# Second expert layer: the seventh product before the sixth and third, and the first block of hidden units used first

## The chip, the cores and the metric

The kernel runs on one core of a Trainium2 chip. A core has a matrix engine (TensorE, called PE in the profile, with its weight loads as PEld), a vector engine (DVE), a scalar engine (ACT), GpSimd (POOL) and a queue that issues transfers (SP). The metric is the device time of one execution, in microseconds. Three runs of the kernel before gave 748.62 us as their median (748.35 to 753.33).

## The reference

Attention over 2 x 8 heads and 576 positions with a memory term gives 1152 tokens of 512 numbers. A feed-forward layer (512 to 2048 units, squared ReLU, back to 512) follows, and then four experts that all see every token:

```python
x = x @ w_in; g = np.maximum(x, 0)**2; x = g @ w_out
for e in range(4):
    h = np.maximum(x @ w1[e], 0.0)        # 512 -> 1024 units
    out += p[:, e:e + 1] * (h @ w2[e])    # 1024 -> 512
```

The result is float32. The change touches the experts alone.

## The kernel before

The experts are computed in two chunks of tokens: 4 tiles of 128 tokens (chunk 0), then 5 tiles (chunk 1). In each chunk a loop goes over 4 experts and 4 quarters of each expert's hidden units, 32 steps in all, numbered 0 to 31 here; steps 0 to 15 are chunk 0. A quarter has 256 units, in two blocks m = 0 and m = 1 of 128.

The first layer of a step (`up2`, from line 872) is a product of a 2 x 2 block matrix (units by inputs) and a 2 x 2 block matrix (inputs by halves of the tokens) in seven block products instead of eight. Products are numbered 0 to 6. Each is six matmuls of 256 columns (320 in chunk 1), because a float32 operand is held as two float16 parts and three pairings are multiplied (`PASS`). Sums on VectorE and GpSimd join the products: p1 from product 0, u2 from product 4, p5 from product 3, u4 = u2 + p5 (on GpSimd), and then
- h[0], the first block of units: its left half is product 1 + p1, its right half product 6 + u4;
- h[1], the second block: its right half is product 5 + u4, its left half product 2 + u3, where u3 is product 5 + u2.

When both halves of a block are there, `hidden(m)` (line 895) makes its two float16 parts: ReLU on ScalarE (L898), then on VectorE the rest (L899), both named g. The order of the products before is 0, 1, 4, 3, 5, 2, 6; I call them by place, U1 to U7. So block 1 is finished after U6 and block 0 after U7.

The second layer of a step (`down2`, line 959) takes g as weights: per token tile and block three matmuls of 512 columns into the bank `o` of that tile (L975), accumulated over the four quarters of an expert and then drained to a sum by VectorE (`drain`, L986/L988). Before, it takes block 1 for all tiles first and then block 0: eight groups D1 to D8 in chunk 0, ten in chunk 1.

The main loop (after line 999) runs the second layer of step i - 1 among the first layer of step i. TensorE's order is the written order: U1 U2 D1 U3 D2 D3 U4 D4 U5 D5 D6 U6 D7 U7 D8 in chunk 0, then U1 of the next step. So g of step i - 1 is first needed at D1, two products after the end of step i - 1. In the last product of step 0 the last groups of the layer ahead (y, L670) stand in place of the D groups; its four blocks are copied out by ScalarE (L676) and VectorE (L677) before the banks can become `o`.

The products of the first layer go round through accumulation banks (`spots`, line 750): four of them in chunk 0, three in chunk 1. A bank is free when ScalarE or VectorE has read the product. Now and then a small product (`yt`, `wt`) takes a place in that round.

ScalarE, VectorE, GpSimd and SP don't run in written order: a scheduler puts the instructions of each engine in a row when the program is built, and each engine runs its row strictly in order. In these rows also stand the splitting of the next weights (`wu` L847, L852 and L858; `w` L782 and L783; `ws` on GpSimd), the sums of squares (`junk`, L779) that wait for the transfer of a weight block (`raw`, L836), and the preparation of chunk 1's tokens (`xs` and `tt`, one piece at the end of each step from step 5 on). A `raw` buffer is loaded again when the split of the block in it has been made.

Of the kernel before, what the change touches and what calls it, by code (L numbers as in the profile page):

```python
# [52 lines left out]
def attention_then_experts(ctx, tc, qa, ka, va, qc, kc, vc, mz, beta, w1, probs, w2, out):  # L53
# [698 lines left out]
    def bank(shape, name):  # L752
        turn[0] += 1
        pool, tag = spots[turn[0] % len(spots)]
        return pool.tile(shape, F32, tag=tag, name=name)
# [116 lines left out]
    def up2(i):  # L872

        c = pairs[i][0]
        n = width[c]
        w = wus.pop(i)

        def product(k):
            acc, x = bank([P, n], "pe"), xs[c][k]
            m = 0  # L880
            for kk in range(2):
                for wa, xb in PASS:
                    nc.tensor.matmul(  # L883
                        acc, lhsT=w[:, wa, k, kk * P:kk * P + P], rhs=x[:, xb, kk], start=(m == 0), stop=(m == 5)
                    )
                    m += 1
            return acc

        def term(tag):
            return xp.tile([P, n], F32, tag=tag, name=tag, bufs=1)  # L890

        h = [xp.tile([P, 2, n], F32, tag=f"h{m}", name=f"h{m}", bufs=1) for m in range(2)]
        p1, p5, u2, u3, u4 = (term(tag) for tag in ("p1", "p5", "u2", "u3", "u4"))

        def hidden(m):
            g = gs[i, m] = xp.tile([P, 2, 2 * n], F16, tag=f"g{m}", name=f"g{m}")
            hm = h[m].rearrange("p j n -> p (j n)")
            nc.scalar.activation(out=g[:, 0], in_=hm, func=AF.Relu)  # L898
            nc.vector.scalar_tensor_tensor(  # L899
                out=g[:, 1], in0=hm, scalar=0.0, in1=g[:, 0], op0=ALU.max, op1=ALU.subtract  # L900
            )

        def add(out, acc, x):
            nc.vector.scalar_tensor_tensor(out=out, in0=acc, scalar=HID, in1=x, op0=ALU.mult, op1=ALU.add)  # L904

        nc.scalar.activation(out=p1, in_=product(0), func=AF.Copy, scale=HID)
        yield
        add(h[0][:, 0], product(1), p1)
        yield
        add(u2, product(4), p1)  # L910
        yield
        nc.scalar.activation(out=p5, in_=product(3), func=AF.Copy, scale=HID)  # L912
        nc.gpsimd.tensor_add(u4, u2, p5)  # L913
        yield
        acc = product(5)
        add(u3, acc, u2)
        add(h[1][:, 1], acc, u4)
        yield
        add(h[1][:, 0], product(2), u3)
        hidden(1)  # L920
        yield
        add(h[0][:, 1], product(6), u4)
        hidden(0)
        yield

    def chain(*gens):
# [3 lines left out]
    with tc.tile_pool(name="ps_3", bufs=1, space=PSUM) as ps_3, tc.tile_pool(name="gp2", bufs=2) as gp2:  # L930
        side, up_0 = chain(tokens(0, nc.gpsimd), prep_up(0)), None
        for i, _ in enumerate(ffn1(2, ps_3, gp2, 2)):
            if i == 6:
                y_power(0, ps_e.tile([P, NK], F32, tag="b", name="yt"))
            if 8 <= i < 56 and i % 4 == 0:
                fetch((i - 8) // 8, i // 4 % 2)
            if 36 <= i < 84 and i % 6 == 0:
                square((i - 36) // 12, i // 6 % 2)
            if i == 90:
                w_power(0, ps_e.tile([P, 8], F32, tag="d", name="wt").rearrange("p (m n) -> p m n", m=2))  # L940
            if (16 <= i < 72 and i % 8 == 7) or (i >= 104 and i % 4 == 3):
                next(side, None)
            if i >= 8 * n1 - 8:
                up_0 = up_0 or up2(0)
                next(up_0, None)
        run(up_0)
# [12 lines left out]
    def down2(i):  # L959

        c, e, p = pairs[i]
        t0, t1 = EXPERT_CHUNKS[c]
        if p == 0:
            scale = prs[c, e] = acp.tile([P, t1 - t0], F32, tag="prs", name="prs", bufs=2)
            nc.vector.tensor_scalar(
                out=scale, in0=pr[:, t0:t1, e], scalar1=winv[:, e:e + 1], scalar2=ypow[:, c, 1:2], op0=ALU.mult, op1=ALU.mult
            )
            for t in range(t0, t1):
                outs[t] = ps_o.tile([P, DM], F32, tag=f"o{t - t0}", name="o")
        todo = [(t, m) for m in (1, 0) for t in range(t0, t1)]  # L970
        for t, m in todo:
            g, w = gs[i, m], wds[i, m]
            r = (t - t0) * P
            for k, (wa, gb) in enumerate(PASS):
                nc.tensor.matmul(  # L975
                    outs[t], lhsT=g[:, gb, r:r + P], rhs=w[:, wa],
                    start=(p == 0 and m == 1 and k == 0), stop=(p == 3 and m == 0 and k == 2),
                )
            if p == 3 and m == 0:
                drain(t, e, t - t0, prs[c, e][:, t - t0:t - t0 + 1])  # L980
            yield

    def drain(t, e, i, scale):
        if e == 0:
            acc[t] = acp.tile([P, DM], F32, tag=f"acc{i}", name="acc")
            nc.vector.tensor_scalar_mul(acc[t], outs[t], scale)  # L986
        else:
            nc.vector.scalar_tensor_tensor(  # L988
                out=acc[t], in0=outs[t], scalar=scale, in1=acc[t], op0=ALU.mult, op1=ALU.add
            )  # L990
        if e == ne - 1:
            r = 0
            for b, r0, n in TILES[t]:
                nc.sync.dma_start(out=out[b * S + r0:b * S + r0 + n, :], in_=acc[t][r:r + n])
                r += n
# [4 lines left out]
    for i in range(len(pairs)):  # L1000
        if pairs[i][0] and len(spots) > 3:
            spots.pop()

        fetch(i + 6, 0)
        fetch(i + 6, 1)
        todo = iter([(j, half) for j in {0: (), 1: (4, 5), 2: (6, 7)}.get(i, (i + 5,)) for half in range(2)])
        if i:
            late = [down2(i - 1)] * (2 * (EXPERT_CHUNKS[pairs[i - 1][0]][1] - EXPERT_CHUNKS[pairs[i - 1][0]][0]))
            steps = spread([up2(i)] * 7, late, 0.25)
        else:  # L1010
            steps = []
        ahead = chain(prep_down(i), prep_up(i + 1))
        for n, g in enumerate(steps):
            next(g)
            next(ahead, None)
            if n in (5, 7, 9, 11):
                square(*next(todo, (len(pairs), 0)))
            if n == 10 and i == 1:
                y_power(1, bank([P, NK], "yt"))
                side = tokens(1, nc.vector)  # L1020
            if n == 14 and i < 4 * ne - 4 and i % 4 == 2:
                w_power(pairs[i + 2][1], bank([P, 8], "wt").rearrange("p (m n) -> p m n", m=2))
        if i >= 5 and steps:
            next(side, None)
        run(ahead)
    run(down2(len(pairs) - 1))


# [58 lines left out]
```

## Time and profile before

| | |
|---|---|
| median of three runs | 748.62 us |
| the profiled execution, its own time | 746.23 us |
| its span, first to last instruction | 744.4 us |
| granted TensorE clock, mean | 0.968 |
| TensorE busy | 698.9 us, 94% of the span |
| VectorE busy | 581.7 us, 78% |

The span is 1.83 us shorter than the execution's own time, which holds what lies around it. The experts take the span from about 371 us on; chunk 0 ends at about 538 us. In the views, "idle before" is the time that an engine stood still ahead of an instruction, and the name behind the arrow is what came last. Overlapping rows of one engine are pipelined.

### The profile page before, as it was taken

How to read it: one execution, taken by the hardware profiler on the slowest of the kernel's cores; microseconds unless marked ns; L12 is line 12 of the kernel's file. 1: busy time of each engine (PE TensorE's matmuls, PEld its weight loads, DVE VectorE, ACT ScalarE, POOL GpSimd, SP SyncE). 2: the span in 40 equal slices, each digit the busy share in tenths (PEclk: the TensorE clock that was granted, in tenths of full speed). 3: DMA queues.
4: the chain of work that ended last, by engine and by line, in shares of the span. 5: the costliest groups of instructions: out<-in, count | busy, mean ns of one | idle time of the engine just before them, and what ended most of it. 6: DMA issues, size and time to landing. Idle time of an engine off the chain costs nothing.

```text
span 744.4 us, 12986 instructions
## 1 busy us (share of the span) xinstructions
PE 698.9 (94%) x4732; PEld 507.2 (68%) x4732; DVE 581.7 (78%) x1081; ACT 449.4 (60%) x888; POOL 295.5 (40%) x293
## 2 busy tenths in 40 slices
PE   8588999989899999989999989999999999999997
PEld 6487978967677887979876555656655555555553
DVE  5888989689989865666788879989787686867763
ACT  5798798686665545687775657645545353535341
POOL 1235536564533237745634243444323323141400
PEclk6779999999999999999999999999999999999999
DMA  8786675187975544685413223223342322100002
GB/s 301 223 302 234 215 240 199 62 283 217 205 190 121 121 114 93 233 291 162 135 59 114 86 85 114 91 81 114 114 148 81 112 70 100 58 1 1 1 1 71
DMA packets 65424, 101.28 MB, mean 136 GB/s; under 512 B 32656, under 2 KB 34704, under 8 KB 65360
## 3 DMA queue, kind: packets, MB, share of 16 engines
q1 hardware_dynamic: 65216, 100.45, 43.2%
q8 instruction: 37, 0.61, 0.3%
q14 instruction: 27, 0.22, 0.1%
q10 hardware_dynamic: 144, 0.00, 0.0%
HBM read 82.87 MB, written 10.75 MB: 126 GB/s over the span
## 4 chain that ended last, share of the span: by engine, by line
PE 35%; DVE 8%; ACT 4%; DMA 3%; issue 3%; POOL 2%; SPq 0%; DVEq 0%; POOLq 0%; ACTq 0%
PE o L975 18%; PE pe L883 16%; DMA raw<-in_w 2%; DVE wu L847 2%; DVE g L899 1%; DMA wraw<-w1s 1%; DVE h L904 1%; ACT junk L779 1%; DVE w L783 1%; POOL w L83 1%; ACT g L898 1%; ACT wu L852 1%; ACT w L82 1%; PE y L670 0%; DVE xs L783 0%
## 5 line engine op out<-in xcount | busy, mean ns | idle before, releaser
L975 PE MATMUL o<-w,g 128*128 128x512 f16 x864 | 219.5, 381 | 6.4 <-DVE g L899 3.9
L883 PE MATMUL pe<-xs,wu 128*128 128x256 f16 (+1 forms) x1344 | 198.6, 288 | 1.8 <-DVE h L904 1.8
L883 PEld LDWEIGHTS <-wu 128*128 128x128 f16 x1344 | 131.8, 99 | 71.0 <-issue 4.2
L975 PEld LDWEIGHTS <-g 128*128 128x128 f16 x864 | 84.1, 98 | 77.6 <-DVE g L899 6.8
L670 PE MATMUL y<-g,w 128*128 128x256 f32 (+2 forms) x576 | 125.3, 351 | 1.4 <-POOL w L83 0.7
L83 POOL TENSOR_TENSOR w<-wraw,w 128x512 fp32r<-128x512 f32 x49 | 72.6, 1485 | 100.8 <-ACT w L82 99.9
L898 ACT ACTIVATE g<-h 128x512 f16<-128x512 f32 (+1 forms) x64 | 43.4, 678 | 107.5 <-DVE h L904 107.4
L670 PEld LDWEIGHTS y<-g,w 128*128 128x128 f32 x576 | 94.5, 191 | 12.0 <-POOL w L83 0.9
L913 POOL TENSOR_TENSOR u<-u,p 128x256 f32<-128x256 f32 (+1 forms) x32 | 31.5, 986 | 135.2 <-ACT p L912 126.7
L899 DVE SCALAR_TENSOR_TENSOR g<-h,g 128x512 f16<-128x512 f32 (+1 forms) x64 | 50.8, 793 | 21.5 <-ACT g L898 21.3
L850 POOL TENSOR_TENSOR ws<-raw 128x256 f32<-128x256 f32 x32 | 23.9, 746 | 99.6 <-issue 86.6
L904 DVE SCALAR_TENSOR_TENSOR h<-pe,u 128x256 f32<-128x256 f32 (+1 forms) x96 | 43.0, 451 | 21.6 <-PE pe L883 16.2
L89 PE MATMUL hpb<-xy,w 128*128 128x512 f32 x192 | 52.9, 412 | 4.9 <-DVE r L660 4.8
L847 DVE SCALAR_TENSOR_TENSOR wu<-ws,wpow,wu 128x512 f16<-128x512 f32 x64 | 52.0, 850 | 3.2 <-ACT wu L858 3.1
L783 DVE SCALAR_TENSOR_TENSOR w<-raw,wpow,w 128x512 f16<-128x512 f32 x64 | 48.2, 755 | 0.7 <-ACT w L782 0.6
L172 DVE CUSTOM_DVE_ANT_0 a<-sc,mask 128x384 f32<-128x384 f32 (+4 forms) x80 | 36.4, 477 | 13.5 <-PE sc L275 7.9
L82 ACT ACTIVATE w<-wraw 128x512 fp32r<-128x512 f32 x64 | 39.5, 622 | 10.6 <-PE y L670 6.9
L89 PEld LDWEIGHTS hpb<-xy,w 128*128 128x128 f32 x192 | 36.1, 196 | 14.1 <-DVE r L660 6.6
L782 ACT ACTIVATE w<-raw,wpow 128x512 f16<-128x512 f32 x64 | 45.0, 709 | 0.5 <-PE o L975 0.5
L83 POOL TENSOR_TENSOR w<-bits,w 128x512 fp32r<-128x512 f32 x24 | 35.3, 1477 | 20.8 <-ACT w L82 17.5
L89 PE MATMUL hpa<-xy,w 128*128 128x256 f32 x192 | 37.3, 320 | 6.0 <-DVE xy L200 3.7
L779 ACT ACTIVATE junk<-raw 128x1024 bf16<-128x1024 f32 x32 | 33.5, 1048 | 14.8 <-DMA raw<-in_w 14.7
(161 smaller groups left out, 1264.6 us busy)
## 6 DMA issues: line engine op xcount, KB each, us to landing
raw<-in_w SPq DMA_DIRECT2D x64, 512.0 KB, 3.3
w<-in_w SPq DMA_DIRECT2D x32, 512.0 KB, 4.1
wraw<-w1s SPq DMA_DIRECT2D x64, 256.0 KB, 2.9
w1s<-bits SPq DMA_DIRECT2D x32, 256.0 KB, 2.5
kraw<-in_kc SPq DMA_DIRECT2D x8, 576.0 KB, 4.2
vraw<-in_vc SPq DMA_DIRECT2D x8, 320.0 KB, 3.6
qraw<-in_qc SPq DMA_DIRECT2D x4, 512.0 KB, 4.7
out<-acc SPq DMA_DIRECT2D x8, 256.0 KB, 2.1
```

Of the source, the lines that this page charges most:

```text
L82: nc.scalar.activation(out=w[:, 0], in_=raw, func=AF.Copy)
L83: eng.tensor_sub(w[:, 1], raw, w[:, 0].bitcast(F32))
L89: nc.tensor.matmul(acc, lhsT=w[:, a, kk * P:(kk + 1) * P], rhs=xy[:, b, kk, t0:t0 + n], start=(i == 0), stop=(i == 3 * NK - 1),)
L670: nc.tensor.matmul(yacc[d], lhsT=w[:, a, d * P:(d + 1) * P], rhs=g[:, b], start=(f == 0 and i == 0 and d % per == 0), stop=(f == n1 - 1 an ...
L782: nc.scalar.activation(out=w0, in_=x, func=AF.Copy, scale=s)
L783: nc.vector.scalar_tensor_tensor(out=w1, in0=x, scalar=s, in1=w0, op0=ALU.mult, op1=ALU.subtract)
L847: nc.vector.scalar_tensor_tensor(out=w[:, 1, ks], in0=x, scalar=s1, in1=w[:, 0, ks], op0=ALU.mult, op1=ALU.subtract)
L883: nc.tensor.matmul(acc, lhsT=w[:, wa, k, kk * P:kk * P + P], rhs=x[:, xb, kk], start=(m == 0), stop=(m == 5))
L898: nc.scalar.activation(out=g[:, 0], in_=hm, func=AF.Relu)
L899: nc.vector.scalar_tensor_tensor(out=g[:, 1], in0=hm, scalar=0.0, in1=g[:, 0], op0=ALU.max, op1=ALU.subtract)
L904: nc.vector.scalar_tensor_tensor(out=out, in0=acc, scalar=HID, in1=x, op0=ALU.mult, op1=ALU.add)
L975: nc.tensor.matmul(outs[t], lhsT=g[:, gb, r:r + P], rhs=w[:, wa], start=(p == 0 and m == 1 and k == 0), stop=(p == 3 and m == 0 and k == 2),)
```

## The change

Product 6, with the add that finishes h[0] and with `hidden(0)`, is taken in the fifth place; products 5 and 2 follow. The order of the products is 0, 1, 4, 3, 6, 5, 2. The second layer takes block 0 for all tiles first and then block 1, and the flags that open and close the accumulation, and the place of the drain, go with it. No instruction is added or removed.

```diff
         nc.gpsimd.tensor_add(u4, u2, p5)
         yield
+        add(h[0][:, 1], product(6), u4)
+        hidden(0)
+        yield
         acc = product(5)
         add(u3, acc, u2)
         add(h[1][:, 1], acc, u4)
         yield
         add(h[1][:, 0], product(2), u3)
         hidden(1)
         yield
-        add(h[0][:, 1], product(6), u4)
-        hidden(0)
-        yield
...
-        todo = [(t, m) for m in (1, 0) for t in range(t0, t1)]
+        todo = [(t, m) for m in (0, 1) for t in range(t0, t1)]
...
-                    start=(p == 0 and m == 1 and k == 0), stop=(p == 3 and m == 0 and k == 2),
+                    start=(p == 0 and m == 0 and k == 0), stop=(p == 3 and m == 1 and k == 2),
                 )
-            if p == 3 and m == 0:
+            if p == 3 and m == 1:
```

The scheduler makes other rows of it. VectorE at the end of step 0, where the layer ahead ends (pe_4472, pe_4486, pe_4488 and pe_4502 are products of step 0, y0 to y3 the four blocks of the layer ahead, wu_4607 the next weights but one), before:

```order
L904 SCALAR_TENSOR_TENSOR h1_4418<-pe_4472,u4_4423 128x256
L677 TENSOR_TENSOR xy_75<-y0_3696,xy_75 128x384
L904 SCALAR_TENSOR_TENSOR h1_4418<-pe_4486,u3_4422 128x256
L677 TENSOR_TENSOR xy_75<-y1_3697,xy_75 128x384
L899 SCALAR_TENSOR_TENSOR g1_4494<-h1_4418,g1_4494 128x512
L904 SCALAR_TENSOR_TENSOR h0_4417<-pe_4502,u4_4423 128x256
L677 TENSOR_TENSOR xy_75<-y2_3698,xy_75 128x384
L677 TENSOR_TENSOR xy_75<-y3_3699,xy_75 128x384
L899 SCALAR_TENSOR_TENSOR g0_4510<-h0_4417,g0_4510 128x512
```

and with the change:

```order
L904 SCALAR_TENSOR_TENSOR h0_4417<-pe_4472,u4_4423 128x256
L899 SCALAR_TENSOR_TENSOR g0_4480<-h0_4417,g0_4480 128x512
L677 TENSOR_TENSOR xy_75<-y0_3696,xy_75 128x384
L904 SCALAR_TENSOR_TENSOR u3_4422<-pe_4488,u2_4421 128x256
L904 SCALAR_TENSOR_TENSOR h1_4418<-pe_4488,u4_4423 128x256
L677 TENSOR_TENSOR xy_75<-y1_3697,xy_75 128x384
L904 SCALAR_TENSOR_TENSOR h1_4418<-pe_4502,u3_4422 128x256
L847 SCALAR_TENSOR_TENSOR wu_4607<-raw0_3864,wpow_3677,wu_4607 128x768
L899 SCALAR_TENSOR_TENSOR g1_4510<-h1_4418,g1_4510 128x512
L677 TENSOR_TENSOR xy_75<-y2_3698,xy_75 128x384
L677 TENSOR_TENSOR xy_75<-y3_3699,xy_75 128x384
```

The subtractions of y2 and y3 now stand behind a weight split (wu_4607) and behind the second block's g; before, only adds and the first g stood there. The first matmul of step 0's second layer waits, in both programs, for VectorE's count up to the subtraction of y3.

ScalarE from step 5's p5 on (junk is a sum of squares that waits for the transfer of raw0_5208; p1_5214 is of step 6), before:

```order
L912 ACTIVATE p5_5081<-pe_5141 128x256
L779 ACTIVATE junk2_3680,wsq_3679<-raw0_5208 128x1024
L898 ACTIVATE g1_5177<-h1_5079 128x512
L779 ACTIVATE junk2_3680,wsq_3679<-raw1_5210 128x1024
L782 ACTIVATE w0_5227<-raw1_4548,wpow_3677 128x512
L898 ACTIVATE g0_5191<-h0_5078 128x512
L906 ACTIVATE p1_5214<-pe_5219 128x256
```

and with the change:

```order
L912 ACTIVATE p5_5081<-pe_5141 128x256
L898 ACTIVATE g0_5162<-h0_5078 128x512
L779 ACTIVATE junk2_3680,wsq_3679<-raw0_5208 128x1024
L779 ACTIVATE junk2_3680,wsq_3679<-raw1_5210 128x1024
L898 ACTIVATE g1_5191<-h1_5079 128x512
L906 ACTIVATE p1_5214<-pe_5219 128x256
```

The g that step 6's second layer begins with stood behind the sum of squares on raw0_5208 and now stands in front of it; the other g and p1 of step 6 stand behind two such sums now, where one stood before.

VectorE in step 10 from the fifth product on (pe_5788 is the fifth product in both; xs12 is a split of chunk 1's tokens), before:

```order
L904 SCALAR_TENSOR_TENSOR u3_5723<-pe_5788,u2_5722 128x256
L904 SCALAR_TENSOR_TENSOR h1_5719<-pe_5788,u4_5724 128x256
L783 SCALAR_TENSOR_TENSOR xs12_5199<-tt_5712,ypow_3676,xs12_5199 128x640
L904 SCALAR_TENSOR_TENSOR h1_5719<-pe_5803,u3_5723 128x256
L899 SCALAR_TENSOR_TENSOR g1_5811<-h1_5719,g1_5811 128x512
L904 SCALAR_TENSOR_TENSOR h0_5718<-pe_5817,u4_5724 128x256
```

and with the change:

```order
L904 SCALAR_TENSOR_TENSOR h0_5718<-pe_5788,u4_5724 128x256
L783 SCALAR_TENSOR_TENSOR xs12_5199<-tt_5712,ypow_3676,xs12_5199 128x640
L899 SCALAR_TENSOR_TENSOR g0_5796<-h0_5718,g0_5796 128x512
L904 SCALAR_TENSOR_TENSOR u3_5723<-pe_5805,u2_5722 128x256
L904 SCALAR_TENSOR_TENSOR h1_5719<-pe_5805,u4_5724 128x256
L904 SCALAR_TENSOR_TENSOR h1_5719<-pe_5817,u3_5723 128x256
```

Both adds that free the bank of product 5 stood in front of xs12. Now the one add on the fifth product stands in front of it, and the two adds on product 5, which is the sixth, stand behind xs12 and behind the first g.

## Rows read from the trace of the kernel before

**Rows 1.** The page, busy time by engine: busy us, share, instructions.
```profile
PE 698.9 (94%) x4732; PEld 507.2 (68%) x4732; DVE 581.7 (78%) x1081; ACT 449.4 (60%) x888; POOL 295.5 (40%) x293
```

**Rows 2.** Waits of PE, 330 to 745 us: total us, times, longest.
```profile
PE o L975 <- DVE g L899: 3.9, 7, 1.3
PE o L975 <- ACT g L898: 2.5, 3, 1.3
PE pe L883 <- DVE h L904: 1.8, 4, 0.8
```

**Rows 3.** Windows: length, busy PE, PEld, DVE, ACT, POOL, clock, DMA share, GB/s.
```profile
518.74:528.50 9.76, 9.76 (x67) 6.46 (x66) 7.56 (x15) 5.11 (x9) 4.86 (x6) 1.00 0.30 108
...
408.61:442.40 33.79, 30.48 (x202) 19.40 (x201) 25.30 (x44) 21.26 (x37) 9.96 (x13) 1.00 0.26 86
430.42:442.40 11.98, 10.36 (x70) 6.66 (x69) 8.62 (x15) 7.57 (x13) 2.90 (x4) 1.00 0.21 66
442.40:467.59 25.19, 22.07 (x133) 13.33 (x132) 24.91 (x48) 19.69 (x33) 12.21 (x14) 0.93 0.27 95
453.88:467.59 13.71, 11.95 (x67) 6.97 (x66) 13.43 (x24) 11.17 (x19) 7.72 (x9) 0.88 0.31 111
467.59:487.15 19.56, 19.56 (x133) 12.83 (x132) 19.53 (x31) 10.56 (x18) 8.78 (x8) 1.00 0.32 108
487.15:508.98 21.83, 20.44 (x137) 13.04 (x136) 19.70 (x42) 10.59 (x18) 9.76 (x13) 1.00 0.29 98
...
600.00:660.00 60.00, 60.00 (x356) 34.57 (x354) 44.14 (x73) 25.71 (x40) 18.95 (x25) 1.00 0.21 71
```

**Rows 4.** Timeline of VectorE and ScalarE: start, us, instruction, idle before.
```profile
418.65 0.42 DVE L904 SCALAR_TENSOR_TENSOR h<-pe,u 128x256 f32<-128x256 f32 x1 [2.61 <-POOL u L913]
431.45 1.06 ACT L779 ACTIVATE junk<-raw 128x1024 bf16<-128x1024 f32 x1 [5.59 <-DMA raw<-in_w]
487.71 1.06 DVE L783 SCALAR_TENSOR_TENSOR xs<-tt,ypow,xs 128x640 f16<-128x640 f32 x1 [0.23 <-ACT xs L782]
```

**Rows 5.** Timeline of PE in chunk 0, matmuls that waited and those behind.
```profile
433.18 0.39 PE L975 MATMUL o<-w,g 128*128 128x512 f16 x1 [1.28 <-ACT g L898]
445.63 0.60 PE L975 MATMUL o<-w,g 128*128 128x512 f16 x2 [1.02 <-DVE g L899]
457.66 0.77 PE L975 MATMUL o<-w,g 128*128 128x512 f16 x2 [1.26 <-DVE g L899]
458.22 1.49 PE L883 MATMUL pe<-xs,wu 128*128 128x256 f16 x6
489.15 0.82 PE L883 MATMUL pe<-xs,wu 128*128 128x256 f16 x6 [0.81 <-DVE h L904]
500.73 0.61 PE L975 MATMUL o<-w,g 128*128 128x512 f16 x2 [0.24 <-DVE g L899]
```

**Rows 6.** Timeline of all engines where the experts' second layer begins.
```profile
375.89 0.49 ACT L676 ACTIVATE xy<-y 128x384 fp32r<-128x384 f32 x1 [1.36 <-PE y L670]
378.50 0.86 ACT L676 ACTIVATE xy<-y 128x384 fp32r<-128x384 f32 x2
379.07 1.01 DVE L677 TENSOR_TENSOR xy<-y,xy 128x384 fp32r<-128x384 f32 x2
380.14 0.81 PE L975 MATMUL o<-w,g 128*128 128x512 f16 x3
381.04 0.95 ACT L852 ACTIVATE wu<-raw,wpow 128x768 f16<-128x768 f32 x1
382.02 1.02 DVE L847 SCALAR_TENSOR_TENSOR wu<-raw,wpow,wu 128x768 f16<-128x768 f32 x1
```

**Rows 7.** The page, costliest groups: one group's busy time, mean ns, idle before.
```profile
L899 DVE SCALAR_TENSOR_TENSOR g<-h,g 128x512 f16<-128x512 f32 (+1 forms) x64 | 50.8, 793 | 21.5 <-ACT g L898 21.3
```

**Rows 8.** Timeline of VectorE and GpSimd in step 7.
```profile
443.72 1.30 POOL L851 TENSOR_TENSOR ws<-ws,raw 128x256 f32<-128x256 f32 x1
444.36 1.21 DVE L899 SCALAR_TENSOR_TENSOR g<-h,g 128x512 f16<-128x512 f32 x1
447.50 0.68 DVE L899 SCALAR_TENSOR_TENSOR g<-h,g 128x512 f16<-128x512 f32 x1
```

## The prediction, made before the changed kernel had run

> **What bounds the kernel now.** The page gives TensorE 94% of the span [rows 1], so time can only come out of TensorE's gaps. The list of TensorE's waits from 330 us on gives them by cause: 3.9 and 2.5 us in which a second-layer matmul waited for g, and 1.8 us in which a first-layer matmul waited for VectorE to free a bank [rows 2]. That is 8.2 us, 1.1% of the time, and the first two, 6.4 us, are what the change aims at. Where they lie is read from the windows, one row per stretch of whole steps [rows 3]. A step of chunk 0 that waits for nothing lasts 9.76 us (518.74 to 528.50). Against that, steps 4 to 6 (408.61 to 442.40) lose 33.79 - 29.28 = 4.5 us, steps 7 and 8 lose 25.19 - 19.52 = 5.7, steps 9 and 10 nothing, steps 11 and 12 lose 21.83 - 19.52 = 2.3. That makes 12.5 us, of which two small `wt` products are about 0.5. In chunk 1 TensorE is busy for 60.00 of 60 us [rows 3]: there the change has nothing to win, and only something to lose.
>
> The same rows show two regimes. In steps 4 to 6 VectorE works 25.30 of 33.79 us; it stands still too, so these waits are latency, a late link in a chain. In steps 7 and 8 it works 24.91 of 25.19 us, in 9 and 10 19.53 of 19.56: there VectorE is the bound, and TensorE follows at a distance that the banks and the g buffers set. The waits themselves are in the timeline of TensorE [rows 5]: 1.28 us at 433.18, 1.02 at 445.63, 1.26 at 457.66, each at D1, the first use of g in a step; and a first-layer product at 489.15 that waited 0.81 for a bank.
>
> **The change part by part.** The work is the same. Three things move.
>
> *Block 0's g comes two products earlier and is used at the same place.* Before, from the end of U6 to D1 stand U7, D7, D8, U1 and U2: 3 x 0.65 + 2 x 0.65 = 3.2 us, 0.65 being a step's 9.76 us over its 15 groups. The add, ReLU and second part of g need about 0.4 + 0.65 + 0.8 = 1.9 us with VectorE's g at 793 ns [rows 7] and the add and the ReLU estimated from it. So VectorE may lag 1.3 us before D1 waits. After, from the end of U5 to D1 stand nine groups less one, 5.2 us: a lag of 3.3 us is borne. Block 1's g is due at D5 of the next step, at least as late as block 0's was. So D1's waits go wherever VectorE's lag stays under about 3 us. The next limit is then a bank: the fifth product's bank is freed by one add, the sixth's by two, behind g on VectorE.
>
> *Steps 4 and 5: -2.3 us.* Their 4.5 - 2.2 us (the window of step 6 alone is 11.98) are latency. At 418.65 VectorE had waited 2.61 us for u4, and at 431.45 ScalarE stood 5.59 us at a sum of squares whose block was still coming, with g behind it [rows 4]. In the new order p5 and the first g stand ahead of these sums. I take all of it; bounds 0 and 2.3.
>
> *Step 6: 0.* The second g and p1 of step 6 now stand behind two sums of squares. The block must wait for VectorE's split of its predecessor in step 5, so it lands at about the time it does now; p1 then comes some 1.5 us later than TensorE would like, VectorE stands still for it, and the 2.2 us of step 6 turn from a wait for g into waits for banks. Bounds: -1.9 (all but `wt`) and +1.
>
> *Steps 7 to 10.* VectorE is the bound, and its row holds the same work in both kernels, so its own progress does not change. TensorE runs ahead by what the longer lag allows: 3.3 - 1.3 = 2.0 us. On top of it, in step 8 the granted clock was 0.88 in the mean, and six matmuls after the wait at 457.66 took 1.49 us [rows 3, 5]; TensorE was busy 11.95 us there instead of 9.76. Of these 2.2 us I count 1.0 as won if the clock stays at its upper level, since VectorE worked on through them. I take -3.0; bounds 0 and -5.7. A rule speaks of this clock: the Trainium skill (TensorE: Matmul & The Clock Gate, Part 1: The HAM clock gate) has the low clock as the state of an engine that has been idle, which activity lifts. This trace agrees, with the drop at 1.2 GHz right behind the waits of steps 7 and 8.
>
> *Step 11 gives most of it back: +2.5 us.* A lead is kept only while banks come free. In step 10 VectorE's new row puts the split xs12 (1.06 us, [rows 4]) and the first g (0.8) in front of the two adds that free the sixth product's bank, and with a `wt` product in the round the second product of step 11 needs that bank. VectorE starts xs12 at 487.71 as before; 1.06 + 0.8 + 2 x 0.35 gives 490.2 at most, or 489.2 with VectorE half a us ahead, where that product started at 489.15 before [rows 5]. So TensorE stands there at the old time again. Bounds: +1.5 and +3.5.
>
> *Steps 11 and 12, D1's small waits: -0.5.* The 0.24 at 500.73 [rows 5] and the like of step 11 go; the rest of the 2.3 us is banks and `wt` and stays.
>
> *The start of the second layer: +2.4 us.* This is the cost that the diff does not show. The first matmul of D1 in step 1 began at 380.14, right after VectorE ended the last subtraction of the layer ahead, 379.07 + 1.01 = 380.08 [rows 6]; it waits for that, not for g. In the new rows ScalarE's weight split (0.95 us) stands ahead of the copy of y2 and VectorE's (1.02) and a g ahead of the subtractions; before, both splits ran at 381.04 and 382.02, when D1 was on its way [rows 6]. The first g moves into the 1.36 us in which ScalarE stood idle at 375.89, and pushes that copy some 0.4 us back. Then ScalarE's split starts at 378.9 instead of the copy at 378.50 and ends at 379.9; VectorE's split ends at 380.9, g at 381.6, the two subtractions at 382.6. That is 2.5 us behind 380.08, and some of it may be hidden by pipelining. Bounds: 0.9 (ScalarE's split alone) and 3.0.
>
> The sum: +2.4 - 2.3 + 0 - 3.0 + 2.5 - 0.5 = **-0.9 us**. I add -0.3 for the last bank waits at the turn to chunk 1, which are of the same kind as those in rows 2 and small: **-1.2 us**. Against the profiled execution's 746.23 us that is 745.0; that execution lies 2.4 us under the median of the runs, 748.62, so the median forecast is **747.4 us**.
>
> **The rivals.**
>
> *A: the waits go and nothing takes their place.* VectorE has room over the whole of steps 4 to 12 (25.30 + 64.1 us of work in 100.4), and if its row packs better than I replay it, the lead is kept through step 11 and step 6 is won too. Then 2.3 + 1.9 + 5.7 + 1.5 = 11.4 us go and 2.4 come at the start: -9.0, or 739.6 us; with half of steps 7 and 8 it is -6.1, 742.5. For it: the aim fits the list of waits, whose greatest item is g. Against: VectorE at 99% in steps 7 to 10.
>
> *B: slower, by the start.* The 2.4 us at 380 are a mechanism with one place: D1 of step 1 behind a weight split that was moved ahead of y3's subtraction. If steps 4 to 8 are bound by VectorE alone (its rows in 7 to 10 say so for these), the lead is lost by step 11 and latency turns into bank waits in steps 4 and 5 as well, so the start is all that remains: +2 to +3, 750.9 us. It decides from the point where less than 2.4 us is won in steps 4 to 12.
>
> *C: g meets GpSimd.* Beside a GpSimd addition of 1.30 us a g took 1.21 us, three us later, alone, 0.68 [rows 8]. The first g now follows u4 and the `ws` sums of GpSimd directly. Were it met in each of the six VectorE-bound steps, 7 to 12, these would each be 0.53 us longer: 3.2 us, against the -1.2 of the forecast +2.0, 750.6 us. The Trainium skill (SBUF — State Buffer, SBUF: two separate sides) has VectorE with two SBUF inputs and GpSimd exclude each other on a shared port, instruction by instruction; g has two such inputs, and the row at 444.36 agrees. Against it: one g of the two already falls there now, as its mean of 793 says.
>
> That the change doesn't do what it says is not a case by itself: the rows of the built program show block 0's g first on every engine, though the scheduler's other moves are the costs above.
>
> **How the numbers follow.** Chances: forecast 0.52 (745 to 749.5), A 0.20, B 0.18, C 0.10. The range, 741.5 to 751.0, takes in the forecast, B, C and the milder half of A. One per cent is 7.5 us, and about what a measurement of this kernel can tell from no change. Faster by that needs nearly all of A: 0.10. Slower by that, 756 us, needs B and C together and a chunk 1 that no longer runs without waits: 0.03. Within 1%: 0.87.
>
> **What would show it.** Right: D1 of step 1 starting some 2 us later behind L677, with the splits ahead of it; waits of L975 for g down from 6.4 us to under 1.5; waits of L883 for `h` on VectorE up from 1.8 to 4 or more; no window of step 8 under a clock of 0.95; VectorE still busy all through steps 7 to 10; step 13 starting within 3 us of 508.98. Wrong: D1 of step 1 at 380.2; bank waits that stay under 2 us, with a step 13 that starts 5 us earlier; or any wait in chunk 1.

## The result: slower by 0.7%

With the change the kernel takes 753.86 us (median of 19 runs, 751.15 to 755.82), before it 748.05 (19 runs on the same chip): a ratio of 1.0072, 95% interval 1.0059 to 1.0086, or 5.4 us more. The forecast was 747.4 with a range to 751.0; sign and size are wrong, and the time lies outside the range. The profiled execution took 751.15 us, 4.9 more than that of before.

TensorE's waits from 330 us on, by cause (us in total, times, longest), with the change:

```profile
PE pe L883 <- DVE h L904: 11.4, 10, 2.6
PE o L975 <- DVE xy L677: 2.0, 1, 2.0
PE o L975 <- DVE g L899: 1.2, 3, 0.5
```

The waits for g that the change aimed at are nearly gone: 6.4 us before [rows 2], 1.2 now. In their place first-layer products wait for a bank (`h`) 11.4 us instead of 1.8, and the start waits 2.0. Step 1 by itself and steps 2 to 12 as one stretch, before and then with the change (start:end, length, busy time of each engine, granted clock, DMA share, GB/s):

```profile
378.61:388.95 10.34, 10.30 (x72) 6.91 (x72) 9.53 (x27) 7.25 (x16) 3.83 (x5) 1.00 0.16 54
388.95:508.98 120.03, 112.21 (x734) 71.73 (x733) 105.73 (x198) 74.26 (x124) 47.86 (x55) 0.99 0.28 97
```

```profile
378.32:390.75 12.43, 10.43 (x72) 6.88 (x72) 8.48 (x21) 8.21 (x19) 3.53 (x5) 1.00 0.16 45
390.75:513.91 123.16, 111.77 (x733) 72.07 (x732) 108.85 (x205) 74.60 (x124) 52.68 (x55) 0.99 0.29 95
```

Step 1 is 2.09 us longer, steps 2 to 12 are 3.13 longer; after that nothing of weight is added. The third busy column is VectorE's. In steps 2 to 12 it stands still for 120.03 - 105.73 = 14.30 us before and for 123.16 - 108.85 = 14.31 us now. So the stretch is longer by just what VectorE is busy longer, 3.12 us. That the two agree so closely is in part chance, since in single steps VectorE has room (in step 3 it is busy 9.54 of 10.91 us with the change, in step 6 9.65 of 13.06). Where the longer busy time comes from shows in its groups over the same stretch (count, busy us, mean ns), before and with the change:

```profile
L899 DVE SCALAR_TENSOR_TENSOR g<-h,g 128x512 f16<-128x512 f32 x22 | 17.0, 773 | 8.0 <-ACT g L898 7.9
L783 DVE SCALAR_TENSOR_TENSOR xs<-tt,ypow,xs 128x640 f16<-128x640 f32 x7 | 6.3, 906 | 0.2 <-ACT xs L782 0.2
```

```profile
L899 DVE SCALAR_TENSOR_TENSOR g<-h,g 128x512 f16<-128x512 f32 x22 | 18.9, 858 | 8.4 <-ACT g L898 8.3
L783 DVE SCALAR_TENSOR_TENSOR xs<-tt,ypow,xs 128x640 f16<-128x640 f32 x7 | 6.9, 1000 | 0.6 <-ACT xs L782 0.6
```

The same number of g, 22, takes 1.9 us more, the seven splits of tokens 0.6 more. Some 1.05 us of work came over from step 1 (9.53 busy before, 8.48 now), and other groups are a little shorter.

How TensorE meets this is seen where step 7 begins. TensorE's timeline with the change (start, length, matmuls, idle before and releaser), and below it VectorE's:

```profile
443.89 0.28 PE L761 MATMUL wt<-wsq,ones 128*128 128x8 f32 x2
445.33 0.82 PE L883 MATMUL pe<-xs,wu 128*128 128x256 f16 x6 [1.16 <-DVE h L904]
448.28 1.07 PE L883 MATMUL pe<-xs,wu 128*128 128x256 f16 x6 [2.13 <-DVE h L904]
449.14 1.49 PE L975 MATMUL o<-w,g 128*128 128x512 f16 x3
450.42 1.49 PE L883 MATMUL pe<-xs,wu 128*128 128x256 f16 x6
```

```profile
442.14 1.01 DVE L847 SCALAR_TENSOR_TENSOR wu<-raw,wpow,wu 128x768 f16<-128x768 f32 x1
443.07 1.88 DVE L847 SCALAR_TENSOR_TENSOR wu<-ws,wpow,wu 128x512 f16<-128x512 f32 x2
444.87 0.41 DVE L904 SCALAR_TENSOR_TENSOR h<-pe,u 128x256 f32<-128x256 f32 x1
445.20 1.23 DVE L783 SCALAR_TENSOR_TENSOR xs<-tt,ypow,xs 128x640 f16<-128x640 f32 x1
446.35 1.21 DVE L899 SCALAR_TENSOR_TENSOR g<-h,g 128x512 f16<-128x512 f32 x1
447.48 0.41 DVE L904 SCALAR_TENSOR_TENSOR u<-pe,u 128x256 f32<-128x256 f32 x1
447.81 0.74 DVE L904 SCALAR_TENSOR_TENSOR h<-pe,u 128x256 f32<-128x256 f32 x2
```

The first product of step 7 needs the bank of step 6's fifth product; the one add that frees it is the row at 444.87, and it stands behind three weight splits. `wt` has taken a place in the round of four banks, so the second product of step 7 needs the bank of step 6's sixth product. That bank is free when u3 and the right half of h[1] are added, and both adds stand behind a token split and the first g. The first of the two `h` rows at 447.81 is the second of these adds; by the 0.41 us of such an add it ends at about 448.22, and TensorE starts at 448.28. Then the clock drops: 1.49 us for six matmuls that take 0.82.

### The profile page after: what moved, and what is told of

Read it like the earlier page. It is cut to its first block, busy times and chain, and to the rows that moved or that the text cites. A ratio compares the mean times of both kernels' runs of the same rounds, so it can differ in the third digit from the quotient of the medians.

```text
span 749.3 us, 12988 instructions
## 1 busy us (share of the span) xinstructions
PE 695.3 (93%) x4732; PEld 504.6 (67%) x4732; DVE 580.6 (77%) x1081; ACT 449.5 (60%) x888; POOL 303.1 (40%) x293
## 4 chain that ended last, share of the span: by engine, by line
PE 35%; DVE 8%; ACT 2%; DMA 2%; issue 2%; POOL 1%; DVEq 0%; ACTq 0%; POOLq 0%; SPq 0%
PE o L975 19%; PE pe L883 16%; DMA raw<-in_w 2%; DVE wu L847 2%; DVE g L899 1%; DVE w L783 1%; DVE h L904 1%; DVE acc L988 1%; DVE xs L783 1%; ACT g L898 1%; ACT junk L779 1%; DVE u L904 1%; POOL u L913 0%; ACT wu L852 0%; ACT w L782 0%
## 5 line engine op out<-in xcount | busy, mean ns | idle before, releaser
L883 PE MATMUL pe<-xs,wu 128*128 128x256 f16 (+1 forms) x1344 | 197.9, 287 | 12.0 <-DVE h L904 11.4
L899 DVE SCALAR_TENSOR_TENSOR g<-h,g 128x512 f16<-128x512 f32 (+1 forms) x64 | 52.4, 819 | 23.7 <-ACT g L898 23.0
L852 ACT ACTIVATE wu<-raw,wpow 128x768 f16<-128x768 f32 x32 | 29.8, 932 | 42.3 <-PE pe L883 40.7
L89 PE MATMUL hpc<-xy,w 128*128 128x384 f32 x192 | 38.5, 345 | 4.9 <-POOL w L83 2.5
```

The lines of the kernel that those rows point to most:

```text
L89: nc.tensor.matmul(acc, lhsT=w[:, a, kk * P:(kk + 1) * P], rhs=xy[:, b, kk, t0:t0 + n], start=(i == 0), stop=(i == 3 * NK - 1),)
L883: nc.tensor.matmul(acc, lhsT=w[:, wa, k, kk * P:kk * P + P], rhs=x[:, xb, kk], start=(m == 0), stop=(m == 5))
L899: nc.vector.scalar_tensor_tensor(out=g[:, 1], in0=hm, scalar=0.0, in1=g[:, 0], op0=ALU.max, op1=ALU.subtract)
```

## The experiments

Each ran beside the kernel before. Differences to the change are differences of the two ratios, times 748 us; where I give a ±, it is worked out from the two intervals. "Stretch" is steps 6 to 11.

**1 and 2: each suspected cause undone by itself.** A helper `behind(x, y)` pins instruction x behind y in its engine's row, without a wait; `held[-1]` are the last copy and the last subtraction of y, `later` is put around all splits of step 2's weights, and x below is step 0's second g. Theory T (two causes: the start, and the sixth product's bank, freed behind the first g), its rivals and the later theories T2 and T' are stated in the expectations.

```diff
-        nc.scalar.activation(out=w[:, 0, 0:3], in_=u[:, 1:4], func=AF.Copy, scale=s1)
+        later(nc.scalar.activation(out=w[:, 0, 0:3], in_=u[:, 1:4], func=AF.Copy, scale=s1), 0)
...
+        def later(ins, k):
+            if i == 2:
+                behind(ins, held[-1][k])
...
+        if i == 0:
+            behind(x[0], held[-1][0])
+            behind(x[1], held[-1][1])
```

> The change, with ScalarE's and VectorE's split of step 2's weights, and step 0's second g, put behind the copies and subtractions of the four blocks y; nothing else moves in the rows but what stands next to these. Theory T (two causes: the start, and the bank of the sixth product, whose two adds now stand behind the first g in VectorE's row): D1 of step 1 starts at about 380.2 instead of 381.94 and the 2.0 us wait for L677 is gone; the time falls by 1.5 to 2.0 us against the change, to 1.004 to 1.005 of the kernel before; the waits of first-layer products for h in steps 3, 7, 9 and 11 stay, 9 to 12 us in all. Rival 1 (VectorE's work beside GpSimd sets the pace in steps 6 to 11, whatever the order of its row): starting earlier is lost again by step 11, and the time falls by 0 to 0.5 us.

Measured: 1.0044 of the kernel before (1.0027 to 1.0061), 2.1 us ± 1.6 under the change. Step 1 lasts 11.00 us instead of 12.43:

```profile
378.51:389.51 11.00, 10.42 (x71) 6.87 (x70) 9.31 (x26) 7.83 (x19) 4.08 (x5) 1.00 0.16 51
```

A wait of 0.6 for L677 remains, since the first g still pushes ScalarE's copies back. The start is a cause, at about the size that the prediction gave it. Waits for h stay (9.8 us).

```diff
-        hidden(0)
+        g0 = hidden(0)[1]
         yield
         acc = product(5)
         add(u3, acc, u2)
-        add(h[1][:, 1], acc, u4)
+        x = add(h[1][:, 1], acc, u4)
+        if i:
+            behind(g0, x)
```

> The change, with the first g of each step from step 1 on put behind the sixth product's two adds in VectorE's row. T: the bank comes free earlier by one g and ScalarE's round trip; the waits for h in steps 3 (0.98), 5 and 6 (0.5, 0.8), 9 (0.7) go, those in step 7 (1.16 and 2.13) and step 11 (0.83 and 2.60) fall by about 1.2 each; 11.4 us of waits for h becomes 4 to 7, the waits of D1 for g grow by less than 1 us, and the time falls by 3 to 5 us against the change, to about 1.002 of the kernel before or just under it. Rival 1: VectorE has the same work, so the waits for h turn into waits for g; the time stays within 1 us of the change. Rival 3 (the adds are late because u4 comes late from GpSimd, so h0's add holds the row up, not g): the waits fall by less than a third, the time by 0 to 1.5 us.

Measured: 1.0028 (1.0014 to 1.0041), 3.3 us ± 1.4 under the change, inside the 3 to 5 that T said. But the waits mostly moved: those for h fell to 6.7 us, as T said, and those for g rose from 1.2 to 5.0, where T had less than 1 us more:

```profile
PE pe L892 <- DVE h L914: 6.7, 6, 1.3
PE o L987 <- DVE g L908: 5.0, 5, 1.6
PE o L987 <- DVE xy L686: 2.0, 1, 2.0
```

TensorE waits 13.7 us in these three lines, against 14.6 with the change. What fell is VectorE's busy time in steps 2 to 12, from 108.85 to 106.62 us, with g at 769 ns (so the edit also takes g away from GpSimd), and the stretch at the low clock, of which this profile has none:

```profile
392.01:513.32 121.31, 110.28 (x733) 71.23 (x732) 106.62 (x201) 74.66 (x124) 52.90 (x55) 1.00 0.30 96
```

So T was right on the time and only in part on its reason, and rival 1 was right that waits for h turn into waits for g. From here on I held theory T2: VectorE sets the pace.

**3: both edits.**

> The change with both edits: step 2's weight split and step 0's second g behind the four blocks y, and from step 1 on the first g behind the sixth product's two adds. If the two causes add, the 1.44 us shorter first step and the gain of the second edit (1.0028 against 1.0072) stand side by side: 1.000 of the kernel before, between 0.998 and 1.002. Theory T2 (formed from the runs so far: in steps 6 to 11 VectorE sets the pace; the stretch lasts 4.6 to 5.5 us more than VectorE is busy in it, in five kernels alike): a start of TensorE that is 1.4 us earlier lets VectorE start earlier too, so it says the same. Rival (the gains overlap): no better than the better of the two, 1.002 to 1.003.

Measured: 0.9992 (0.9973 to 1.0011), 6.0 us ± 1.7 under the change. Within this accuracy the two causes add (2.1 and 3.3 us) and make up the whole loss.

**4 and 5: the round of banks shifted in every step.**

```diff
+            if n == 14 and i < 4 * ne and not (i < 4 * ne - 4 and i % 4 == 2):
+                turn[0] += 1
```

> The change, with one place of the bank round left empty at the end of every step 1 to 15 that has no small product wt there; no instruction is added and every engine's row is the same. So each step's second product needs the bank of the sixth product of the step before, as after a wt. T: waits for h also come up in steps 4 to 6, 8 to 10 and 12, 0.5 to 2 us each; 11.4 us of such waits becomes 15 to 20 and the time rises by 3 to 8 us against the change. Rival 1: nothing in the rows changes and VectorE sets the pace: within 1 us of the change.

> The kernel before with the same empty places in the bank round; every engine's row is that of the kernel before. Rival 2 (the shift of the round by itself costs the time, whichever product comes sixth): it rises as much as with the change, 3 to 8 us. T: the sixth product has one add there, and no g stands ahead of it: waits for h rise from 1.8 to at most 4 us, the time by 0 to 2 us.

Measured: 1.0050 (1.0033 to 1.0067) on the change, 1.6 us ± 1.6 less than it and not more; 0.9981 (0.9967 to 0.9994) on the kernel before. With the change, waits for h rose to 14.7 us, just under what T said, up to this one in step 9,

```profile
473.56 0.81 PE L883 MATMUL pe<-xs,wu 128*128 128x256 f16 x6 [3.14 <-DVE h L904]
```

but waits for g went to nothing, and the time did not rise. T's second number and rival 2 both fell: making TensorE wait for that bank in more steps does not by itself cost time.

**6, 7 and 8: room on VectorE.** `if i >= 5 and steps` becomes `if i >= 2 and steps`: chunk 1's tokens are prepared three steps earlier, where VectorE has idle time.

> The kernel before, with chunk 1's tokens (xs, tt) prepared from step 2 on instead of step 5. T2: 13.9 us of VectorE's 63.27 us in steps 6 to 11 are this work; nearly half of it falls into steps 2 to 5, where VectorE stands still for 8 us. The stretch of steps 6 to 11 falls from 68.4 to 62 to 65 us, steps 2 to 5 rise by 0 to 2, the time falls by 3 to 5 us: 0.994 to 0.996 of the kernel before. T (waits are latency of a late link): 0 to 1 us less.

> The change, with chunk 1's tokens prepared from step 2 on. T2: the change's 3.5 us in steps 6 to 11 are VectorE's longer busy time (63.27 to 66.39 us) there; with room on VectorE they go, and what remains against the kernel before with the same edit is the start, 2.0 to 2.5 us. T (two adds behind the first g, whatever VectorE's load): the difference to the kernel before with the same edit stays at 4 to 5.4 us.

> Both edits of the rows and the tokens from step 2 on, with the change's order of products. T2: no start loss, no D1 waits in steps 4 to 6, VectorE with room in 6 to 11: 0.990 to 0.995 of the kernel before, 0 to 3 us under the kernel before with the tokens early. T: 0.997 to 1.000.

Measured: 0.9940 (0.9920 to 0.9960), 0.9972 (0.9953 to 0.9991) and 0.9916 (0.9888 to 0.9943), all three in T2's ranges. Steps 2 to 12, of the kernel before with the edit and then of the change with it:

```profile
387.67:504.50 116.83, 110.88 (x734) 71.87 (x733) 105.97 (x199) 75.77 (x125) 47.46 (x55) 0.99 0.31 100
```

```profile
391.67:507.39 115.72, 109.99 (x734) 71.45 (x733) 105.98 (x199) 74.58 (x124) 50.41 (x55) 1.00 0.32 101
```

The change's 3.13 us in steps 2 to 12 are gone (it is 1.1 us shorter there now, at 0.9 less TensorE time). What remains between the two is 2.4 us ± 2.1, the size of the start. The third kernel, with the change's order of products, is 741.42 us and faster than both kernels; against the kernel before with the tokens early it is 0.24% ± 0.34 faster, so that the change's order of products, with its two causes undone, is worth nothing that these runs can tell.

**9 and 10: GpSimd's sums nearly taken away.** The four sums ws are made over k columns (`k = 2 * P if i < 6 or pairs[i][0] else 8`); both kernels leave out the sums over the other columns, in chunk 0 from the weights of step 6 on.

> The kernel before; from step 5 to the end of chunk 0 GpSimd's four sums ws of a step are made over 8 columns instead of 256 (the rest keeps an earlier step's values), so VectorE meets nothing of GpSimd there but u4. It is the base for the next run. T2 with rival C: g, xs and the splits of ws shorten; VectorE's busy time in steps 6 to 11 falls from 63.3 to 58 to 61 us and the time by 2 to 4 us. If the meeting costs nothing, both stay.

> The change with the same thin sums. If the change's longer VectorE time in steps 6 to 11 (66.39 against 63.27 us) comes from g and xs meeting GpSimd's sums, the mean g there falls from 903 ns to that of the base (within 30 ns), VectorE's busy time comes within 0.8 us of the base, and the two kernels differ by the start alone, 2 to 3 us. Rival T (two adds behind the first g): g may be equal, but waits for h stay at 8 us or more and the difference at 4 to 5.4 us.

Measured: 0.9927 (0.9906 to 0.9948), 5.5 us less than before, and 1.0007 (0.9991 to 1.0023). g over steps 2 to 12, in the one and in the other:

```profile
L901 DVE SCALAR_TENSOR_TENSOR g<-h,g 128x512 f16<-128x512 f32 x22 | 15.1, 687 | 9.1 <-ACT g L900 9.1
```

```profile
L901 DVE SCALAR_TENSOR_TENSOR g<-h,g 128x512 f16<-128x512 f32 x22 | 15.3, 698 | 9.0 <-ACT g L900 8.9
```

The longer g is GpSimd's doing: 773 and 858 ns become 687 and 698. The Trainium skill (SBUF — State Buffer, SBUF: two separate sides) has a VectorE instruction with two SBUF inputs, as g is, and a GpSimd instruction that reads SBUF exclude each other on a shared port; these rows agree. But the loss did not go with it. The two kernels differ by 6.0 us ± 2.0, where T2 said 2 to 3 and T 4 to 5.4, and the change still waits 8.7 us for h, as T said it would. In steps 2 to 12 it is 1.95 us longer than its base, though VectorE is busy alike:

```profile
388.91:505.75 116.84, 110.60 (x733) 71.02 (x732) 101.05 (x199) 73.53 (x123) 29.05 (x55) 1.00 0.31 100
```

```profile
392.94:511.73 118.79, 110.32 (x734) 71.43 (x732) 100.83 (x197) 74.22 (x124) 31.87 (x55) 1.00 0.30 98
```

So in the traces about 1.2 of the 3.13 us hang on GpSimd, and about 2 remain with the changed order of VectorE's row. T2 alone does not cover the second part. In the medians the 1.2 do not show. In the profile step 1 makes up for them: it is 3.62 us longer than the base's 10.32, at a lower clock:

```profile
379.00:392.94 13.94, 11.98 (x72) 7.51 (x72) 10.57 (x28) 8.16 (x17) 3.59 (x5) 0.88 0.14 40
```

**11 and 12: more work for VectorE.** One unused addition of 128x512 is put into each of steps 6 to 11, or into 1 to 4, of the kernel before.

> The kernel before with one more VectorE addition of 128x512 float32 (not used) in each of steps 6 to 11, behind what stood ahead of it in the written order; some 0.7 us each, 4.2 us in all. T2: the stretch of steps 6 to 11 grows by its whole length, 3.5 to 5.5 us, and so does the time (1.005 to 1.007). T (latency of single links): 0 to 1.5 us.

> The control: the same addition in each of steps 1 to 4, where VectorE stands still for 8 of 40 us. T2: 0 to 1 us of the 2.8 us show (0.9995 to 1.0015). A rival in which any VectorE work counts: 2.5 to 3 us.

Measured: 1.0053 (1.0034 to 1.0073), or 4.0 us, and 1.0014 (0.9998 to 1.0030), or 1.0 us and not clear of nothing. The stretch of the kernel before, and with the additions:

```profile
430.42:498.79 68.37, 62.48 (x401) 39.49 (x400) 63.27 (x117) 43.34 (x71) 27.80 (x30) 0.98 0.27 93
```

```profile
433.93:505.84 71.91, 64.03 (x401) 39.98 (x400) 66.68 (x122) 43.44 (x71) 26.82 (x30) 0.95 0.28 88
```

3.41 us more of VectorE make the stretch 3.54 us longer (1.55 of it is TensorE busy longer, with the granted clock at 0.95 instead of 0.98). There VectorE's time counts in full. In steps 1 to 4 less of it counts: VectorE is busy 2.44 us longer over steps 1 to 12 (117.70 and 115.26), and these last 1.4 us longer in the profile, 1.0 in the medians.

**13 to 16: through which bank.** Still open was whether the row costs time through the bank after `wt` (T) or in every step (T').

```diff
+            if n == 1 and i < 4 * ne - 3 and i % 4 == 3:
+                w_power(pairs[i + 1][1], bank([P, 8], "wt").rearrange("p (m n) -> p m n", m=2))
...
-            if n == 14 and i < 4 * ne - 4 and i % 4 == 2:
-                w_power(pairs[i + 2][1], bank([P, 8], "wt").rearrange("p (m n) -> p m n", m=2))
```

> The change, with the small product wt taken after the second product of the next step instead of at the step's end, so that the second product gets the bank of the fifth product (one add, in front of g) in every step. T: the waits for h of the second product in steps 3 (0.98), 7 (2.13) and 11 (2.60) go, 11.4 us of waits for h become 5 to 7, and the time falls by 2 to 4 us against the change (1.002 to 1.0045 of the kernel before). T' (g in front of the adds holds VectorE's chain up in every step, whatever the bank): 0 to 1 us.

> Both edits of the rows, the tokens early and wt later, together: the version that should be best. T: with the adds in front the bank of the sixth product is hardly late, so little is left: 0 to 1.5 us under the version without the last edit, 0.989 to 0.992 of the kernel before.

Measured: 1.0097 (1.0074 to 1.0119) and 1.0009 (0.9995 to 1.0024): worse, by 1.9 us than the change and by 7 us on the best version (experiment 8). The edit was ill made. `wt` itself now comes third and gets the sixth product's bank, and it waits as long as the second product did:

```profile
448.49 0.39 PE L761 MATMUL wt<-wsq,ones 128*128 128x8 f32 x2 [2.14 <-DVE h L904]
496.62 0.39 PE L761 MATMUL wt<-wsq,ones 128*128 128x8 f32 x2 [2.60 <-DVE h L904]
```

The same two numbers, 2.1 and 2.6, for another instruction: the wait belongs to the bank. Besides, the next expert's weights are split later, and products wait for them (0.92 and 0.85 in step 8). As a test of T against T' the pair says nothing more.

The last pair uses the edit of experiment 2 with `if i % 4 == 2`, and with `if i and i % 4 != 2`. Of the first set only steps 2, 6 and 10 end with a `wt` (the condition is `i < 4 * ne - 4`); step 14 does not.

> The change, with the first g behind the sixth product's two adds in steps 2, 6, 10 and 14 alone (the steps that end with wt) and the like of chunk 1. T: most of the 3.3 us that the same edit in all steps gave: 2 to 3.3 us under the change (1.0028 to 1.0045 of the kernel before). T': a quarter of it, 0.5 to 1 us (1.006 to 1.0065).

> The same in all other steps from 1 on, and not in those that end with wt. T: 0 to 1.3 us under the change (1.0055 to 1.0072). T': three quarters of the 3.3 us, 2 to 3 us (1.003 to 1.0045).

Measured: 1.0060 (1.0038 to 1.0083) and 1.0059 (1.0039 to 1.0078), 0.9 and 1.0 us under the change, each ± 1.9. With such an error the pair does not decide between T and T'. In the first of the two the wait at step 7's second product fell from 2.13 to 1.00, by 1.13, about the length of that g (1.21):

```profile
449.43 0.81 PE L892 MATMUL pe<-xs,wu 128*128 128x256 f16 x6 [1.00 <-DVE h L914]
```

So g held that bank; how the 3.3 us divide over the steps stays open.

## Why the prediction was wrong, step by step

Lengths of steps from TensorE's timeline, from first product to first product, so that a wait ahead of a step's first product counts to the step before:

| | forecast us | before | with the change | difference |
|---|---|---|---|---|
| start (step 1) | +2.4 | 10.34 | 12.43 | +2.09 |
| step 3 | 0 | 9.76 | 10.91 | +1.15 |
| steps 4 and 5 | -2.3 | 21.81 | 20.71 | -1.10 |
| step 6 | 0 | 11.98 | 13.06 | +1.08 |
| steps 7 to 10 | -3.0 | 45.13 | 46.30 | +1.17 |
| step 11 | +2.5 | 11.26 | 12.52 | +1.26 |
| step 12, and D1 of 11 | -0.5 | 10.19 | 9.76 | -0.43 |

**The start was right**, in its place and size, and so was its reason. With the change, ScalarE's split, VectorE's split, g and the subtractions, and then D1:

```profile
378.38 0.92 ACT L852 ACTIVATE wu<-raw,wpow 128x768 f16<-128x768 f32 x1
379.20 0.47 ACT L676 ACTIVATE xy<-y 128x384 fp32r<-128x384 f32 x1
379.33 1.02 DVE L847 SCALAR_TENSOR_TENSOR wu<-raw,wpow,wu 128x768 f16<-128x768 f32 x1 [0.26 <-ACT wu L852]
380.26 0.68 DVE L899 SCALAR_TENSOR_TENSOR g<-h,g 128x512 f16<-128x512 f32 x1
380.87 1.02 DVE L677 TENSOR_TENSOR xy<-y,xy 128x384 fp32r<-128x384 f32 x2
381.94 0.81 PE L975 MATMUL o<-w,g 128*128 128x512 f16 x3 [2.00 <-DVE xy L677]
```

Before, the subtractions began at 379.07 and D1 at 380.14 [rows 6]; experiment 1 gives most of it back.

**The step that failed is "Steps 7 to 10", -3.0**, 4.2 of the 6.4 us by which the sum missed. It held that VectorE's row has the same work and keeps its progress, so that TensorE gains the 2.0 us that the longer lag lets it run ahead, and 1.0 of the clock. Steps 7 to 10, before and with the change, and under each the token splits in them:

```profile
442.40:487.53 45.13, 42.01 (x268) 26.47 (x266) 44.77 (x78) 30.63 (x50) 21.38 (x23) 0.96 0.29 100
L783 DVE SCALAR_TENSOR_TENSOR xs<-tt,ypow,xs 128x640 f16<-128x640 f32 x6 | 5.2, 881 | 0.0
445.33:491.63 46.30, 41.84 (x267) 26.55 (x266) 45.55 (x78) 30.00 (x50) 24.09 (x22) 0.96 0.31 101
L783 DVE SCALAR_TENSOR_TENSOR xs<-tt,ypow,xs 128x640 f16<-128x640 f32 x6 | 5.9, 990 | 0.0
```

Both halves were wrong. The same number of VectorE instructions takes 0.78 us longer there, most of it in the token splits; the eight g are hardly longer (7.1 us, before 7.0). And the lead was not there when it was to be used: at the first products of step 7 TensorE stood 1.16 and 2.13 us for banks that VectorE had not freed. Step 8 did lose its waits and its low clock, 9.76 us instead of 13.71, but steps 7, 9 and 10 together grew by 5.12. The text named that limit itself ("the fifth product's bank is freed by one add, the sixth's by two, behind g on VectorE") and then priced it in step 11 alone, where a `wt` and a token split meet. The same `wt` ends steps 2 and 6; the 1.15 in step 3 is the first case, on a VectorE that has room (a wait of 0.98 behind u4 and g). That each wait for a bank adds its length to the time is not shown (experiments 2 and 4); that the loss goes with the first g put behind the adds is (experiments 2 and 3).

**Step 6** went as described, from a wait for g to waits for banks (0.81 us, and the 1.16 ahead of step 7), and came out a little beyond its bound of +1. **Steps 4 and 5** gained half of what was taken: D1's waits went, a bank wait of 0.51 and one of 0.36 for p1 came. **Step 11** had the right mechanism and half the size. **The clock** was counted as 1.0 us won; step 8 has indeed no low clock now (before, it was in step 8 alone, behind the wait at 457.66, and step 7 had 1.00), but step 7 has it:

```profile
445.33:459.06 13.73, 11.60 (x67) 7.08 (x66) 13.11 (x29) 9.05 (x16) 6.73 (x7) 0.88 0.32 109
```

**The rivals.** B (the start is all that remains) had the right sign, and its condition was met: less than 2.4 us was won in steps 4 to 12. C (g meets GpSimd) had a mechanism that is there, but smaller: in the steps 7 to 12 that it named, the mean g went from 843 to 902 ns, about 0.7 us for twelve where I had 3.2 (over steps 2 to 12 it is 1.9). They were kept apart as cases, and the outcome is B's start with a second loss on top, 2.09 + 3.13, of which the longer g is a part; the two together were thought of only for 756 us and more, at 3%.

Of the marks named ahead, D1 of step 1, the waits for g (1.2) and a busy VectorE in steps 7 to 10 came as said; waits for h came at 11.4, nearly three times the 4 named as the least; step 13 began 4.9 us late where 3 was the bound.

What is shown: the two causes, by undoing each and both, and that room on VectorE undoes the second one too (experiments 6 and 7). What stays open: how the second one divides between the longer g and the place of the adds (the traces of 9 and 10 say 1.2 to 2, their medians show no share of g), and over the steps.

## What to carry to other kernels

Before a lead is counted as won, ask on which engine the stretch is full: on a full engine its own busy time counts in full (experiment 11), and a wait taken from one place turns up at another. When an instruction moves forward in a row, list what frees a bank or a buffer behind it, and price that in every step in which the round makes it due, not in one. Two rivals that don't exclude each other must be added before they are weighed.

## What the runs showed of the hardware

From one profile to the next, TensorE's busy time for the same matmuls differs by more than this change, and the granted clock goes with it. Behind the wait of 2.0 us in step 1, in eight profiles that have it, step 1 took 12.42 or 12.43 us three times and 13.94 to 14.11 five times, with the granted clock at 0.88 in the mean of the step (so a part of it at the lower level, half of full speed). In the ten profiles with a shorter wait or none there, the clock stayed at 1.00 in step 1. One of the five, the change with the tokens early:

```profile
377.56:391.67 14.11, 12.11 (x72) 7.46 (x72) 9.71 (x28) 8.33 (x19) 3.53 (x5) 0.88 0.14 40
```

Over steps 1 to 12 the same matmuls kept TensorE busy for 119.72 us in the best version, all at a clock of 1.00, and for 126.36 in the change with `wt` later, at 0.88 in step 1 and 0.97 behind it, by the sums of their steps:

```profile
sum 126.28, PE 119.72 PEld 78.07 DVE 116.90 ACT 82.77 POOL 52.23; mean PE 59.86 PEld 39.04 DVE 58.45 ACT 41.39 POOL 26.12
```

```profile
sum 138.27, PE 126.36 PEld 79.16 DVE 117.05 ACT 82.70 POOL 54.37; mean PE 63.18 PEld 39.58 DVE 58.53 ACT 41.35 POOL 27.19
```

The Trainium skill (TensorE: Matmul & The Clock Gate, Part 1: The HAM clock gate) has the low clock as the state of an engine that has been idle; the rows agree, but the same wait does not always bring it. So a kernel with long single waits pays for them twice in some of its profiles, and the profiles of before and of the change happened to lose about the same by it (122.50 and 122.20 us busy). How much of the spread between runs this makes is not shown: of the 19 runs of the change one took 751.15 us at a mean clock of 0.975, another 755.50 at 0.980.
